# A dynamic convolution and a squared-ReLU feed-forward on one core: the order of the first loads, and block rows copied inside SBUF

## The chip, the cores and the metric

The kernel runs on one core of one Trainium2 chip. A core has five engines, each with its own queue of instructions that it works through in order: TensorE (PE) multiplies matrices, VectorE (DVE) and ScalarE (ACT) do elementwise work, GpSimd (POOL) does elementwise work and issues transfers, SyncE (SP) here issues transfers only. Transfers (DMAs) from SP go through one queue (q1 in the profile), those from POOL through another (q0); both are served by the same 16 DMA engines. SBUF is the on-chip memory with 128 partitions, PSUM is where PE writes, DRAM holds inputs and outputs. The metric is device time in microseconds (us) of one execution; lower is better.

## The reference

```python
# x: (8, 4096, 192), weight_gen: (8, 4096, 8 heads, 7 taps)
w = exp(weight_gen - max);  w = w / (sum(w) + 1e-9)        # softmax over the 7 taps
x_pad = 6 zero rows ahead of each sequence of x
out[b, s, h*24:(h+1)*24] = sum over k of w[b, s, h, k] * x_pad[b, s + k, h*24:(h+1)*24]
# then, on the 32768 rows of out, with w_in (192, 2048) and w_out (2048, 192):
h = maximum(out @ w_in, 0)
return (h * h) @ w_out
```

All inputs are 32-bit floats. The kernel computes in 16-bit floats with 32-bit sums.

## The kernel before

The 32768 rows are worked in 64 blocks of 512 rows (8 blocks to each of the 8 batches). A block goes through these steps:

- *Softmax.* `Softmax` (lines 138 to 210) handles a piece of one batch: `load` brings weight_gen to SBUF, `exp` (L172, ACT), `recip` (L180 and L185, DVE) and `scale` (L193, eight DVE instructions for a small piece) put the normalised taps into a tile `v`, `store` (L207, SP) writes the tile to a DRAM tensor `vd`. Batch 0 is split into three pieces, s0, s1 and s2, of 8, 8 and 16 rows on each of the 128 partitions: rows 0 to 1023, 1024 to 2047 and 2048 to 4095. Their tiles are `v_first[0]` to `v_first[2]`. Later batches are one piece (`v_big`), worked in slices during the blocks before.
- *Rows of taps.* A block's taps are needed in another layout, five tiles of 128 rows each (`wr`), whose tile i begins at row -24 + 104 i of the block. `wr_load` (L264) reads them from `vd` in DRAM; `wr_load_sbuf` (L269) copies them straight from an SBUF tile, one DMA for each of the five.
- *Bands.* `st_band` (L289, DVE) multiplies `wr` with a band mask into `bd`, the banded matrix of the convolution.
- *Convolution.* `st_conv` (L338, PE, 72 small matmuls of x by `bd`) writes `yp` in PSUM, `st_y_evac` (L351, ACT) copies it to SBUF as `y`.
- *Feed-forward.* For each of 8 groups fp: `st_mm1` (L363, 12 matmuls, PE), `st_relu` (L393, ACT), `st_sq` (L399, DVE); then `st_mm2` (L382, PE) with w_out, in two halves, G0 (fp 0 to 3) and G1 (fp 4 to 7). `o_copy` (L404) and `o_store` (L409) bring the result out.

PSUM: three buffers of two banks are shared in turn by the warm-up tile `wp`, `yp` and `h`, so a fourth group of mm1 waits until the first one's relu has read its buffer. `t` (relu's output) has five buffers.

The order of the work is written out by hand: each engine and each DMA queue takes its instructions in the order of the code. The head of the kernel, ahead of the loop over blocks (lines 452 to 495), is: 36 matmuls on zeros (`spin`, L441) while the first data arrive; loads on SP of s0's weights, of both halves of w_in (`load_w_in`, L114 and L115, in f32), of block 0's x (`x_load_f32`); softmax of s0; casts of w_in to f16 into `w_i` (L127: "straight" is slot 0 of the tile, the others are copies of 64 partitions to other slots and partitions) on ACT, POOL and DVE; rows of blocks 0 and 1 copied from s0's SBUF tile; loads of block 1's x and of w_out from POOL; bands and convolution of block 0, four more spins; s1's softmax; s1's store to DRAM; and the load of block 2's rows (`wr_load(2)`) from DRAM, which waits for that store. mm1 of groups 0 to 3 uses the first half of w_in, groups 4 to 7 the second.

In the loop, block 0 runs its groups 0 to 3, then block 1's convolution, block 2's bands, its groups 4 to 7, the first half of mm2, and part of s2's softmax. Block j's other half of mm2 stands in block j+1, behind block j+2's convolution.

Of the kernel before, what the change touches and what calls it, by code (L numbers as in the profile page):

```python
# [9 lines left out]
def kernel(  # L10
# [20 lines left out]
    nc = tc.nc  # L31
# [10 lines left out]
    P = 128  # L42
# [8 lines left out]
    HALO = KK - 1  # L51
# [5 lines left out]
    NT = 5  # L57
# [31 lines left out]
    v_first = [  # L89
        const.tile([P, r + 2 * HALO, HP, SL, 2], f16, name=f"v_first{i}")  # L90
        for i, r in enumerate(FIRST)
    ]
# [17 lines left out]
    def load_w_in(q):  # L110
        c = slice(q * NQ, (q + 1) * NQ)
        w_sa[q] = p_st.tile([P, NQ], f32, name="w_sa")
        w_sb[q] = p_st.tile([RT, NQ], f32, name="w_sb")
        nc.sync.dma_start(out=w_sa[q], in_=moe_w_in[0:P, c])  # L114
        nc.sync.dma_start(out=w_sb[q], in_=moe_w_in[P:D, c])  # L115

    def cast_w_in(q, op, copy):
        c = slice(q * NQ, (q + 1) * NQ)
        lower, upper = slice(0, RT), slice(RT, P)
        out_p, slot, src = {  # L120
            "straight": (slice(0, P), 0, w_sa[q]),
            "up": (upper, 1, w_sa[q][lower]),
            "down": (lower, 1, w_sa[q][upper]),
            "last": (lower, 2, w_sb[q]),
            "last up": (upper, 2, w_sb[q]),
        }[op]
        copy(out=w_i[out_p, slot, c], in_=src)  # L127
# [86 lines left out]
    def new_vd(b):  # L214
        vd_t[b] = p_dr.tile([S, H * SL], f16, name="vd")
        return vd_t[b]


    x_t, wr_t, bd_t, yp_t, y_t, g_t, h_t, t1_t, o_t, o_sb_t = ({} for _ in range(10))
# [32 lines left out]
    def x_load(j):  # L252
        x_t[j] = p_x.tile([P, NT, D], f16, name="xt")
        block_load(j, x_t[j], x[j // NBB], D, nc.gpsimd)
# [9 lines left out]
    def wr_load(j):  # L264
        wr_t[j] = p_wr.tile([P, NT, HP, SL * 2], f16, name="wr")
        wr = wr_t[j].rearrange("p t g c -> p t (g c)")
        block_load(j, wr, vd_t[j // NBB], H * SL, nc.sync)

    def wr_load_sbuf(j, s, order, engines):  # L269

        wr_t[j] = p_wr.tile([P, NT, HP, SL * 2], f16, name="wr")
        for n, i in enumerate(order):
            t0 = max(j * TB + tile_start(j, i), 0)
            engines[n % len(engines)].dma_start(  # L274
                out=wr_t[j][:, i].rearrange("p g c -> p (g c)"),
                in_=s.v[t0 // s.r : (t0 + P) // s.r, HALO : HALO + s.r].rearrange(
                    "p r g c e -> p r (g c e)"
                ),
            )

    def st_band(j, tiles):

# [65 lines left out]
    def st_y_evac(j):  # L348
        y = p_y.tile([P, NK, TH], f16, name="y")
        y_t[j] = y  # L350
        nc.scalar.copy(  # L351
            out=y, in_=yp_t[j][:, 0 : NK * TH].rearrange("p (k c) -> p k c", k=NK)
        )
# [41 lines left out]
    def st_sq(j, fp):  # L395
        g = p_g.tile([P, 2, 2, TH], f16, name="g")
        g_t[(j, fp)] = g
        t1 = t1_t[(j, fp)]
        nc.vector.tensor_tensor(out=g, in0=t1, in1=t1, op=AluOp.mult)  # L399
# [26 lines left out]
    with nc.allow_low_precision("fp16 matmul pipeline"), tc.manual_schedule():  # L426

        vd0 = new_vd(0)
        parts = [
            Softmax(0, P * sum(FIRST[:i]), r, v_first[i], vd0) for i, r in enumerate(FIRST)  # L430
        ]
        warm = const.tile([P, TB], f16, name="warm")
        nc.vector.memset(warm, 0.0)  # L433
        for i in (0, 1):
            nc.vector.memset(v_first[i], 0.0)

        wp = ps_h.tile([P, 2 * TB], f32, name="wp", tag="h")

        def spin(n):
            for i in range(n):  # L440
                nc.tensor.matmul(  # L441
                    out=wp[:, 0:TB], lhsT=warm[:, 0:P], rhs=warm, start=True, stop=True
                )

        def softmax(s, lo, hi):
            s.exp(lo, hi)
            s.recip(lo, hi)
            s.scale(lo, hi, nc.vector)

        vec, act, pool = nc.vector.tensor_copy, nc.scalar.copy, nc.gpsimd.tensor_copy  # L450
        s0, s1, s2 = parts
        spin(36)
        band_mask()
        s0.load(nc.sync)
        load_w_in(0)
        load_w_in(1)
        x_load_f32(0)
        s0.exp(0, s0.rh)
        s0.recip(0, s0.rh)
        s0.scale(0, s0.rh, nc.vector)  # L460
        cast_w_in(0, "straight", act)
        cast_w_in(0, "up", act)
        cast_w_in(0, "down", pool)
        cast_w_in(0, "last", act)
        cast_w_in(0, "last up", act)
        wr_load_sbuf(0, s0, (0, 1, 2, 4, 3), (nc.sync, nc.gpsimd))
        cast_w_in(1, "up", vec)
        cast_w_in(1, "down", vec)
        x_load(1)
        s1.load(nc.sync)  # L470
        for q in range(4):
            load_w_out(q, 4)
        nc.gpsimd.memset(v_first[2], 0.0)
        x_cast(0, act)
        wr_load_sbuf(1, s0, range(NT), (nc.sync,))
        s0.store(nc.sync)
        s2.load(nc.sync)
        cast_w_in(1, "straight", act)
        cast_w_in(1, "last", act)
        for i in (0, 2, 1, 3, 4):  # L480
            st_band(0, (i,))
        st_conv_alloc(0)
        st_conv(0)
        spin(4)
        s1.exp(0, s1.rh)
        st_y_evac(0)
        cast_w_in(1, "last up", act)
        x_load(2)
        nc.gpsimd.memset(v_big, 0.0)
        st_bands(1, 0)  # L490
        st_bands(1, 1)
        s1.recip(0, s1.rh)
        s1.scale(0, s1.rh, nc.vector)
        s1.store(nc.sync)
        wr_load(2)


        plan = {}

        def spread(b, rh, blocks):  # L500
            lo = 0
            for n, j in enumerate(blocks):
                left = len(blocks) - n
                hi = min(lo + -(-(rh - lo) // (UNIT * left)) * UNIT, rh)
                if lo < hi:
                    plan[j] = (b, lo, hi)
                lo = hi

        spread(0, s2.rh, (0, 1))
        for b in range(1, B):  # L510
            first = NBB * (b - 1)
            spread(b, R + HALO, range(first + (2 if b == 1 else -2), first + 5))
        rows_of = {0: s2}

        for j in range(NBLK):
            nb, lo, hi = plan.get(j, (None, 0, 0))
            after = plan.get(j + 1)
            if after and after[1] == 0:
                s = Softmax(after[0], 0, R, v_big, new_vd(after[0]))
                s.load(nc.sync)  # L520
                rows_of[after[0]] = s
            if j + 3 < NBLK:
                x_load(j + 3)

            late = j == 2
            if j:
                if j + 1 < NBLK:
                    st_conv_alloc(j + 1)
                    st_conv(j + 1)
                    st_y_evac(j + 1)  # L530
                if not late:
                    st_bands(j + 2, 0)
            for fp in G0:
                st_mm1(j, fp)
                st_relu(j, fp)
                st_sq(j, fp)
            if j:
                for half in (0, 1):
                    st_mm2(j - 1, G1, (half,))
                    o_copy(j - 1, half, nc.scalar.copy)  # L540
                o_store(j - 1, (0, 1), nc.sync)
            elif NBLK > 1:
                st_conv_alloc(1)
                st_conv(1)
                st_y_evac(1)
                st_bands(2, 0)
            if not late:
                st_bands(j + 2, 1)
            if hi and j:
                s = rows_of[nb]  # L550
                softmax(s, lo, hi)
                if hi == s.rh:
                    s.store(nc.sync)
            for fp in G1:
                st_mm1(j, fp)
                st_relu(j, fp)
                st_sq(j, fp)
            st_mm2(j, G0)
            if hi and not j:
                softmax(rows_of[nb], lo, hi)  # L560
            if late:
                st_bands(j + 2, 0)
                st_bands(j + 2, 1)
            if j + 3 < NBLK:
                wr_load(j + 3)
        st_mm2(NBLK - 1, G1, (0,))
        o_copy(NBLK - 1, 0, nc.scalar.copy)
        st_mm2(NBLK - 1, G1, (1,))
        o_store(NBLK - 1, (0,), nc.sync)
        o_copy(NBLK - 1, 1, nc.vector.tensor_copy)  # L570
        o_store(NBLK - 1, (1,), nc.scalar)
# [30 lines left out]
```

## Time and profile before

| | us |
|---|---|
| median of 4 runs | 794.53 |
| lowest, highest | 792.83, 795.98 |
| the profiled execution | 793.45 |
| its span, first to last instruction | 791.7 |
| PE busy in the span | 772.7 (98%) |
| ACT, DVE, POOL busy | 610.4, 584.5, 73.5 |

A line of a timeline gives the start and the duration in us, the engine, the line of the kernel, the operation, the tile written and the tile read, and how many instructions are merged; the bracket at its end says how long the engine had been idle and what ended that. DMA landings, where a text gives them, are the times at which the DMA's semaphore got its increments from the 16 engines, in the same trace; the last of the 16 counts.

### The profile page before, as it was taken

Reading aid. Unit: us, or ns where it says so; the run is one execution under the profiler, and the core shown is the slowest. Engines: PE = TensorE matmul, PEld = TensorE weight load, DVE = VectorE, ACT = ScalarE, POOL = GpSimd, SP = SyncE. Lnnn points to the kernel's source line nnn. Section 1 sums busy time; section 2 is a strip of 40 time slices with the busy share of each in tenths; the row PEclk is TensorE's granted clock in tenths of the full one; section 3 lists DMA queues with packets and bytes.
Section 4 is the critical chain, followed back from the end, with each engine's and each line's share of the span. In section 5 each row is a group of like instructions: output and inputs, shape, how many; then the busy total and the mean of one; then the engine's idle time right before and its main releaser. Section 6 shows DMA issues by size and latency. Waiting matters only on the chain.

```text
span 791.7 us, 32661 instructions
## 1 busy us (share of the span) xinstructions
PE 772.7 (98%) x14888; PEld 679.3 (86%) x14888; DVE 584.5 (74%) x1042; ACT 610.4 (77%) x761; POOL 73.5 (9%) x96
## 2 busy tenths in 40 slices
PE   7698999999999999999999999999999999999998
PEld 3587888888888888888888988888888888889887
DVE  5688778776887768777778777877778777667653
ACT  6586877877877877877877877877787787787785
POOL 7201000010001000010001000011000010000000
PEclk9899999999999999999999999999999999999999
DMA  9932633435433453435433453333533333342111
GB/s 200 177 78 39 154 55 64 75 51 146 76 52 65 97 110 64 75 52 145 76 51 66 72 133 68 71 54 68 149 61 65 65 64 83 70 70 45 50 42 41
DMA packets 123929, 64.09 MB, mean 81 GB/s; under 512 B 87281, under 2 KB 121104, under 8 KB 123024
## 3 DMA queue, kind: packets, MB, share of 16 engines
q1 hardware_dynamic: 79744, 45.51, 20.8%
q0 software_dynamic: 43776, 16.31, 19.4%
q8 instruction: 116, 1.90, 1.0%
q10 hardware_dynamic: 272, 0.20, 0.1%
q14 instruction: 21, 0.17, 0.1%
HBM read 48.74 MB, written 29.36 MB: 99 GB/s over the span
## 4 chain that ended last, share of the span: by engine, by line
PE 94%; DVE 2%; DMA 2%; SPq 1%; ACT 0%; issue 0%; DVEq 0%
PE o L382 44%; PE h L363 43%; PE yp L338 7%; DMA wr<-v_first 1%; DVE bd L289 1%; SPq L274 1%; DMA vd<-v_first 1%; DVE v_first L193 0%; DMA wg<-in_weight_gen_dram 0%; DVE ssum L180 0%; DVE rcp L185 0%; DVE g L399 0%; ACT ex L172 0%; DMA wr<-vd 0%; DVE v_big L193 0%
## 5 line engine op out<-in xcount | busy, mean ns | idle before, releaser
L393 ACT ACTIVATE t<-h 128x1024 f16<-128x1024 f32 x512 | 482.7, 1030 | 10.4 <-PE h L363 8.3
L399 DVE TENSOR_TENSOR g<-t 128x1024 f16<-128x1024 f16 x512 | 345.1, 690 | 143.8 <-ACT t L393 143.6
L363 PE MATMUL h<-y,w_i 64*128 64x256 f16 x6144 | 361.7, 270 | 0.6 <-ACT t L393 0.3
L382 PE MATMUL o<-w_o,g 128*128 128x192 f16 x4096 | 360.0, 246 | 0.7 <-DVE g L399 0.7
L382 PEld LDWEIGHTS <-g 128*128 128x128 f16 x4096 | 331.5, 98 | 27.6 <-DVE g L399 17.9
L363 PEld LDWEIGHTS <-w_i 64*128 64x128 f16 x6144 | 292.0, 94 | 49.4 <-issue 12.3
L289 DVE TENSOR_TENSOR bd<-wr,mask 128x1664 f16<-128x1664 f16 (+2 forms) x201 | 160.8, 831 | 18.5 <-DMA wr<-vd 12.3
L351 ACT CAST y<-yp 128x768 f16<-128x768 f32 x64 | 51.0, 798 | 121.3 <-PE yp L338 121.3
L250 POOL DMA_DIRECT2D xt<-in_x_dram x63 | 52.1, 828 | 472.9 <-PE yp L338 447.2
L404 ACT COPY o_sb<-o 128x384 f32<-128x384 f32 x127 | 62.9, 495 | 38.2 <-PE o L382 38.0
L338 PE MATMUL yp<-bd,xt 128*32 128x104 f16 (+12 forms) x4608 | 60.6, 203 | 12.6 <-DVE bd L289 9.2
L338 PEld LDWEIGHTS <-xt 128*32 128x32 f16 (+3 forms) x4608 | 51.5, 91 | 23.9 <-issue 20.2
L180 DVE TENSOR_REDUCE ssum<-ex 128x64 f32<-128x448 f32 (+6 forms) x49 | 25.9, 529 | 32.7 <-ACT ex L172 32.7
L193 DVE TENSOR_TENSOR v_big<-ex,rcp 128x112 f16<-128x112 f32 (+3 forms) x192 | 32.8, 235 | 1.6
L172 ACT ACTIVATE ex<-wg 128x448 f32<-128x448 f32 (+6 forms) x49 | 26.5, 541 | 1.9 <-DMA wg<-in_weight_gen_dram 1.9
L185 DVE RECIPROCAL rcp<-ssum 128x64 f32<-128x64 f32 (+6 forms) x49 | 23.3, 476 | 1.7
L244 POOL DMA_DIRECT2D xt<-in_x_dram x10 | 5.7, 575 | 88.4 <-PE yp L338 88.4
L441 PE MATMUL wp<-warm 128*128 128x512 f16 x40 | 11.7, 460 | 1.3 <-DVE warm L433 1.3
L240 POOL DMA_DIRECT2D xt<-in_x_dram x7 | 3.8, 541 | 77.4 <-PE yp L338 77.4
L441 PEld LDWEIGHTS <-warm 128*128 128x128 f16 x40 | 4.3, 112 | 7.4 <-issue 3.2
L193 DVE TENSOR_TENSOR v_first<-ex,rcp 128x112 f16<-128x112 f32 (+2 forms) x32 | 6.3, 270 | 0.2
L127 ACT CAST w_i<-w_sa 128x1024 f16<-128x1024 f32 (+1 forms) x3 | 3.1, 1043 | 1.9 <-DMA w_sa<-in_moe_w_in_dram 1.9
(19 smaller groups left out, 22.9 us busy)
## 6 DMA issues: line engine op xcount, KB each, us to landing
out_dram<-o_sb SPq DMA_DIRECT2D x63, 384.0 KB, 2.8
xt<-in_x_dram POOLq DMA_DIRECT2D x46, 240.0 KB, 4.2
wg<-in_weight_gen_dram SPq DMA_DIRECT2D x6, 1064.0 KB, 5.7
wr<-vd SPq DMA_DIRECT2D x46, 80.0 KB, 3.0
vd<-v_big SPq DMA_DIRECT2D x7, 512.0 KB, 3.3
xt<-in_x_dram POOLq DMA_DIRECT2D x17, 192.0 KB, 3.9
w_sa<-in_moe_w_in_dram SPq DMA_DIRECT2D x2, 512.0 KB, 6.8
wr<-vd SPq DMA_DIRECT2D x16, 64.0 KB, 3.0
```

What stands on the lines that cost most here:

```text
L172: nc.scalar.activation(out=self.ex[:, lo:hi].rearrange("p r g k e -> p (r g) k e"), in_=self.wg[:, lo:hi].rearrange("p r (g e) k -> p (r g ...
L180: nc.vector.tensor_reduce(out=ssum.rearrange("p r g e -> p (r g) e"), in_=self.ex[:, lo:hi].rearrange("p r g k e -> p (r g) e k"), axis=Ax ...
L193: eng.tensor_tensor(out=bass.AP(tensor=v.tensor, offset=v.offset + lo * H * SL + lo % SL * 2 + g * SL * 2, ap=[list(v.ap[0]), [H * SL + 2, ...
L250: eng.dma_start(out=dst[:, first:last], in_=ap)
L289: nc.vector.tensor_tensor(out=bd_t[j][:, H * lo : H * hi].rearrange("p (g m c) -> p g m c", g=shape[1], c=2 * SL), in0=wr_t[j][:, i : tile ...
L338: nc.tensor.matmul(out=yp_t[j][p0 : p0 + m, col + a : col + b], lhsT=x_t[j][:, i, 32 * q : 32 * q + m], rhs=bd[:, h // 2, h % 2, a - lo : ...
L351: nc.scalar.copy(out=y, in_=yp_t[j][:, 0 : NK * TH].rearrange("p (k c) -> p k c", k=NK))
L363: nc.tensor.matmul(out=h[:, half, jj, :], lhsT=w_i[r0 : r0 + RT, slot, fc * P : (fc + 1) * P], rhs=y_t[j][r0 : r0 + RT, k, :], start=(jj = ...
L382: nc.tensor.matmul(out=o[half][:, cc * Dm : (cc + 1) * Dm], lhsT=g_t[(j, fp)][:, half, jj, cc * P : (cc + 1) * P], rhs=w_o[:, fc, :], star ...
L393: nc.scalar.activation(out=t1, in_=h_t[(j, fp)], func=ActF.Relu)
L399: nc.vector.tensor_tensor(out=g, in0=t1, in1=t1, op=AluOp.mult)
L404: copy(out=o_sb_t[j][:, half], in_=o_t[j][half][:, 0 : 2 * Dm])
```

## The change

The first load of x moves ahead of the second half of w_in, and that half's load moves behind the copies of block 0's rows on SP's queue. The copies of block 1's rows move ahead of s1's load. The casts of w_in's second half move behind block 0's evacuation, "straight" on ACT and the four others on POOL. `spin` has 42 matmuls. `wr_load_sbuf` takes several pieces and copies a tile from each piece that it overlaps; block 2's rows are copied with it from s0's and s1's tiles (tile 0 from both, so six DMAs), in place of the load from DRAM. s1's reduce and reciprocal stay in the head; its scale, these copies and its store follow the second square of block 0.

```diff
-    def wr_load_sbuf(j, s, order, engines):
+    def wr_load_sbuf(j, parts, order, engines):
 
         wr_t[j] = p_wr.tile([P, NT, HP, SL * 2], f16, name="wr")
-        for n, i in enumerate(order):
+        n = 0
+        for i in order:
             t0 = max(j * TB + tile_start(j, i), 0)
-            engines[n % len(engines)].dma_start(
-                out=wr_t[j][:, i].rearrange("p g c -> p (g c)"),
-                in_=s.v[t0 // s.r : (t0 + P) // s.r, HALO : HALO + s.r].rearrange(
-                    "p r g c e -> p r (g c e)"
-                ),
-            )
+            for s in parts:
+                a, b = max(t0, s.t0), min(t0 + P, s.t0 + P * s.r)
+                if a < b:
+                    engines[n % len(engines)].dma_start(
+                        out=wr_t[j][a - t0 : b - t0, i].rearrange("p g c -> p (g c)"),
+                        in_=s.v[
+                            (a - s.t0) // s.r : (b - s.t0) // s.r, HALO : HALO + s.r
+                        ].rearrange("p r g c e -> p r (g c e)"),
+                    )
+                    n += 1
...
-        spin(36)
+        spin(42)
         band_mask()
         s0.load(nc.sync)
         load_w_in(0)
-        load_w_in(1)
         x_load_f32(0)
...
         cast_w_in(0, "last", act)
-        cast_w_in(0, "last up", act)
-        wr_load_sbuf(0, s0, (0, 1, 2, 4, 3), (nc.sync, nc.gpsimd))
-        cast_w_in(1, "up", vec)
-        cast_w_in(1, "down", vec)
+        wr_load_sbuf(0, [s0], (0, 1, 2, 4, 3), (nc.sync, nc.gpsimd))
+        load_w_in(1)
         x_load(1)
+        wr_load_sbuf(1, [s0], range(NT), (nc.sync,))
         s1.load(nc.sync)
         for q in range(4):
             load_w_out(q, 4)
-        nc.gpsimd.memset(v_first[2], 0.0)
         x_cast(0, act)
-        wr_load_sbuf(1, s0, range(NT), (nc.sync,))
+        cast_w_in(0, "last up", act)
         s0.store(nc.sync)
         s2.load(nc.sync)
-        cast_w_in(1, "straight", act)
-        cast_w_in(1, "last", act)
         for i in (0, 2, 1, 3, 4):
             st_band(0, (i,))
         st_conv_alloc(0)
         st_conv(0)
         spin(4)
+        st_y_evac(0)
+        cast_w_in(1, "straight", act)
+        cast_w_in(1, "up", pool)
+        cast_w_in(1, "down", pool)
+        cast_w_in(1, "last", pool)
+        cast_w_in(1, "last up", pool)
         s1.exp(0, s1.rh)
-        st_y_evac(0)
-        cast_w_in(1, "last up", act)
+        nc.gpsimd.memset(v_first[2], 0.0)
         x_load(2)
         nc.gpsimd.memset(v_big, 0.0)
         st_bands(1, 0)
         st_bands(1, 1)
         s1.recip(0, s1.rh)
-        s1.scale(0, s1.rh, nc.vector)
-        s1.store(nc.sync)
-        wr_load(2)
+
+        def rest_of_s1():
+            s1.scale(0, s1.rh, nc.vector)
+            wr_load_sbuf(2, [s0, s1], range(NT), (nc.sync,))
+            s1.store(nc.sync)
...
                 st_sq(j, fp)
+                if (j, fp) == (0, 1):
+                    rest_of_s1()
```

## The prediction

> **What bounds the kernel now.** I read the page first: share of busy time, then the chain that ended last.
>
> ```profile
> PE 772.7 (98%) x14888; PEld 679.3 (86%) x14888; DVE 584.5 (74%) x1042; ACT 610.4 (77%) x761; POOL 73.5 (9%) x96
> ...
> PE 94%; DVE 2%; DMA 2%; SPq 1%; ACT 0%; issue 0%; DVEq 0%
> ```
>
> TensorE (PE) is the bound: 94% of the chain is matmuls, and nothing the change touches makes them fewer. What is left for it is the head, where the chain runs over other engines. So next the timeline of the first 40 us (start, duration, instruction, idle before it and who ended that), which shows where PE stands still:
>
> ```profile
> 14.16 1.03 PE L338 MATMUL yp<-bd,xt 128*32 128x104 f16 x26 [3.10 <-ACT xt L262]
> ...
> 22.62 0.56 DVE L289 TENSOR_TENSOR bd<-wr,mask 128x768 f16<-128x768 f16 x1 [2.11 <-DMA wr<-v_first]
> ...
> 23.23 0.44 PE L338 MATMUL yp<-bd,xt 128*32 128x96 f16 x22 [1.06 <-DVE bd L289]
> ...
> 24.98 1.46 DVE L193 TENSOR_TENSOR v_first<-ex,rcp 128x112 f16<-128x112 f32 x8
> ...
> 27.09 2.81 PE L382 MATMUL o<-w_o,g 128*128 128x192 f16 x32 [0.69 <-DVE g L399]
> ...
> 32.70 2.43 DVE L289 TENSOR_TENSOR bd<-wr,mask 128x1664 f16<-128x1664 f16 x3 [3.85 <-DMA wr<-vd]
> ...
> 33.87 0.27 PE L338 MATMUL yp<-bd,xt 128*32 128x104 f16 x2 [3.96 <-DVE bd L289]
> 34.71 1.46 PE L338 MATMUL yp<-bd,xt 128*32 128x56 f16 x70 [0.57 <-DVE bd L289]
> ```
>
> Two holes matter: 3.10 us before block 0's convolution, and 3.96 + 0.57 us before block 2's. The second follows from one path: s1's scale ends at 26.44, its store lands in DRAM at 30.55 (15 of 16 engines at 28.82), the load of block 2's rows is issued at 30.61 and lands at 32.67, then bands. The chain in order of time says the same:
>
> ```profile
> 24.98 1.47 DVE v_first L193 x8
> 26.46 4.09 DMA vd<-v_first
> 30.58 0.03 issue
> 30.61 2.07 DMA wr<-vd
> 32.70 1.97 DVE bd L289 x2
> ```
>
> The stages of this stretch (window: us, PE busy, PEld, DVE, ACT, POOL, granted PE clock, DMA share, GB/s) show a second price of the hole, the clock:
>
> ```profile
> 30.00:32.00 2.00, 0.00 (x0) 0.00 (x0) 0.00 (x0) 0.70 (x1) 0.00 (x0) 1.00 0.17 28
> 32.00:34.00 2.00, 0.13 (x2) 0.14 (x3) 1.30 (x2) 0.00 (x0) 0.00 (x0) 0.59 0.88 120
> 34.00:36.00 2.00, 1.43 (x72) 1.23 (x69) 2.00 (x4) 0.00 (x0) 0.00 (x0) 0.50 0.84 328
> 36.00:38.00 2.00, 2.00 (x29) 1.36 (x20) 2.00 (x4) 1.19 (x2) 0.84 (x1) 0.50 0.40 161
> ```
>
> Block 1's first 48 matmuls of L363 take 4.28 us from 36.11 at half clock; the same 48 take 2.79 at 23.61. From 40.32 on (the product with w_out of block 0's second half) PE has no hole until 63.87, and that one is set by work that starts after an output copy of PE's own. So a shift of 40.32 goes to the end whole, and **the forecast is that shift**.
>
> **The change, part by part.** *x_st before w_in(1).* x_st landed at 13.04, after w_in's second half (11.59); between 8.23 and 11.59 the queue moved that half, 3.4 us. Moved ahead, x_st lands near 9.7 (8.23 + its own 1.45). Block 0's five row copies, issued from 9.20 on, landed 13.22 to 13.94, right behind x_st; with an empty queue they land 2.0 us after issue (as the 2.07 of wr<-vd), at 11.2 to 12.5. Bands (five, 2.57 busy) end near 14.1 instead of 15.89, block 0's convolution ends near 14.5 to 15 instead of 16.66. Gain 1.6 us there, if what follows keeps it.
>
> *spin(42).* Six more matmuls of 0.213 are 1.3 us, from 11.06 to 12.35, inside the hole that remains. Cost nothing; if the bands came before 12.3, at most 1.3.
>
> *w_in(1) now stands on SP's queue behind block 0's copies*, and s1.load, which was issued at 11.18 and landed at 14.70, stands behind w_in(1) and block 1's five copies. This is the term that decides. On ScalarE (ACT), in order, s1.exp stands ahead of block 0's first relu; so that relu waits for s1.load, and behind it the other relus and block 1's evacuation (PE waits for both, for PSUM buffers), and on DVE s1's reduce with the squares behind it. Call the landing L.
> w_in(1) is issued at 11.18, moves from about 12.3 (first load: issued 0.80, moving at 1.9). Alone, 768 KB took 3.4 us; beside POOL's queue (20 to 24 us) SP's queue moved 0.76 MB in 4.0 us. 1.6 us of the one and 2.1 of the other: landed at 16.0. Block 1's five copies took from 14.70 to 20.80 beside w_out and x: 6.1 us. POOL has the same loads to make here (x_load(1) and w_out, 2688 packets; about 630 of them by 16.0, the rest at the 407 per us that it made from 14 to 20), so it runs dry around 21, and I put 5.5 to 6.1: 21.5 to 22.1. s1.load itself: 392 KB, 1.3 us as before or 2.1 at the crowded rate. L = 22.8 to 24.2; I take **23.5**. Ends: copies uncrowded, 0.18 us apart as block 0's were, give 16.0 + 0.9 + 1.3 = 18.2; the slowest engine's lag (1.8 us on the last copy, 20.80 to 22.60, 3.4 on the last w_out piece, 21.58 to 25.02) gives 24.2 + 3.4 = 27.6. I stand by the middle because it is the same five copies against the same queue.
> The Trainium skill, "DMA: Bandwidth & Descriptors", section on queues, rings and completion order, says that each engine takes turns between the queues with work, a packet at a time. The row above it: from 14 to 20 us SP's queue moved 702 packets and POOL's 2440, no equal turns. With equal turns the copies' 640 packets would take some 2.4 us and L would be an estimated 19.8; I keep the row.
>
> *From L on* (durations from the rows): exp 0.93, reduce 0.96, reciprocal 0.85: L + 2.8. Two squares, which the change puts here, 2 x 0.62: L + 4.1 (their relus end by L + 2.9). Scale 1.46: L + 5.6. Six copies for block 2 on SP, 0.64 each (L274 took 0.60 and a gap of 0.04): tile 1, the third, leaves at L + 6.9, lands 2.07 later, L + 9.0; tile 3 at L + 10.3. Bands: 1.0 each, the second ends at L + 11.3, the last at L + 11.9. Convolution of block 2, 0.92 at full clock, ends about L + 12.4; 48 matmuls of L363, 2.79: L + 15.2. POOL's x_load(5), which was done by 28, now falls beside the copies: 0 to 1 us, taken 0.5, since DMA there is otherwise idle. Total L + 15.7 = 39.2, against 40.32: **1.1 us gained**. From scale to convolution's end the new way costs 6.8 instead of 9.7 (36.17 - 26.44); what it gains, s1's late arrival eats: before, the scale ended at 26.44, now at L + 5.6 = 29.1.
> Lag of the last engine on L is likely in part; half its smaller size, 0.9, once in two: 0.4. Net **0.7 us gained**.
>
> *PE beside this.* It stops after three of four mm1 groups of block 0 (three PSUM buffers), near 17.5 to 18, until the relu at L + 1.96: a hole of 7.5 us in place of those above, and the clock falls. In this trace PE restarts at 14.16 and 33.87 got full clock 4.6 and 5.3 us later; so here at L + 7. Rest of mm1 (1.4 cold), convolution of block 1 (1.7 cold), four mm1 groups (one cold, three warm, 3.5), mm2 (2.81): L + 1.96 + 9.4 = L + 11.4, just under the bands' L + 11.9. If the clock came two us later, up to 1.3 us more.
>
> *Casts of w_in(1).* DVE loses two (1.47 us, from idle time), ACT keeps one, POOL gets four, 1.12 each as its one now: from 15 to about 20.5; used at L + 5. Behind them on POOL: v_first memset, x_load(2) (16.69, now about 22.5), v_big memset, x_load(3) (19.91, now about 26); x is needed at 34 and 48; landing takes 3.8. Covered by over 7 us. A POOL cast beside DVE's scale made it 2.30 instead of 1.46; here bands of block 1 run beside, which wait for copies and then for s1 anyway: 0, at worst 0.8.
>
> *SP's tail.* s0.store and s2.load move behind s1.load; s2.exp, at 29.86 before, now comes after L + 10, and 616 KB land by L + 5. s1.store is issued behind the six copies, near L + 9.5; block 3's rows land some 5 us later, bands for it at about 41; batch 1's weights (issued at 32.07, 5.4 to land) leave near 36 and are used at 55.5. All covered by 2 us or more.
>
> **The sum.** The profiled run took 793.45 us (span 791.7 and 1.75 around it): 793.45 - 0.7 = 792.75. The median of four runs is 1.08 higher, so 793.8. A measurement of this kernel tells from no change about 0.3%, 2.4 us.
>
> **Rivals.** *A, faster:* s1.load is not last, because the copies are less crowded (w_out's 1.5 MB is held up by w_in(1), x_load(2) not yet issued). For: POOL's queue runs dry near 21. Against: 6.1 us for the same copies now. With L at 21.0: 21.0 + 15.2 to 15.7 = 36.2 to 36.7, 3.6 to 4.1 us faster, 790.4 to 790.9. It passes 2.4 us at L below 22.2.
> *B, slower:* one DMA engine lags, and s1.load, at the end of the row, waits for it, with relu, squares and block 2 behind it. For: 22.60 against 20.80, 25.02 against 21.58, 30.55 against 28.82. Against: 14.70 and 19.39 landed with their fellows, and the POOL queue drains earlier here. L = 27.5 gives 43.2, 2.9 us slower: 797.4. It decides above L = 27.0.
> *C, nothing of it is seen:* block 2's rows come earlier, but PE's own cold work is the bound: with the clock two us later its mm2 ends at L + 12.7 and the convolution at L + 13.6 instead of 12.4, which makes 0.7 faster into 0.5 slower, inside no change.
>
> **How the numbers follow.** Forecast with C (L 22.2 to 27): 0.52, of its own 792.1 to 796.5. A 0.25, B 0.23. The range runs to the rivals' values, 790.4 to 797.5. Same comes from the forecast, faster from A, slower from B.
>
> **What would show it.** Right: s1.exp released by its DMA near 23.5, relu of block 0 after it; PE idle 7 us before 26; the bands of block 2 released by wr<-v_first at L + 9; full clock at block 1's mm1, 48 in about 2.8. Wrong: s1.exp before 21, or PE waiting for something other than the relu there; copies for block 2 landing later than 4 us after issue; a POOL cast that mm1 waits for.

## The result and the profile after

The changed kernel takes 794.86 us (median of 53 runs) against 793.61 before (79 runs): ratio 1.0018, 95% interval 1.0010 to 1.0026, so slower by some 1.4 us. The forecast was 0.7 us faster and called it no change that can be told; the size is inside that, the sign is not. The 2.4 us that the prediction took for the smallest difference a measurement can tell was too much: with these numbers of runs the interval is 0.6 us to either side.

The page of the kernel after, share of busy time and the chain that ended last:

```profile
PE 772.3 (98%) x14894; PEld 679.1 (86%) x14894; DVE 582.8 (74%) x1040; ACT 608.2 (77%) x759; POOL 77.5 (10%) x100
...
PE 93%; DVE 3%; DMA 2%; issue 1%; SPq 0%; ACT 0%; DVEq 0%
```

PE does the same work. Its chain lost one per cent to DVE and to issue time, all of it in the head. The timeline of the first 45 us, with the lines that answer to those shown of before:

```profile
14.23 0.91 PE L343 MATMUL yp<-bd,xt 128*32 128x104 f16 x46 [0.71 <-DVE bd L294]
...
23.43 0.94 ACT L172 ACTIVATE ex<-wg 128x784 f32<-128x784 f32 x1 [5.49 <-DMA wg<-in_weight_gen_dram]
...
25.33 1.47 PE L368 MATMUL h<-y,w_i 64*128 64x256 f16 x12 [7.15 <-ACT t L398]
...
27.32 1.45 DVE L193 TENSOR_TENSOR v_first<-ex,rcp 128x112 f16<-128x112 f32 x8
...
35.47 2.43 DVE L294 TENSOR_TENSOR bd<-wr,mask 128x1664 f16<-128x1664 f16 x3 [5.50 <-DMA wr<-v_first]
...
36.64 0.23 PE L343 MATMUL yp<-bd,xt 128*32 128x104 f16 x2 [2.37 <-DVE bd L294]
...
37.48 0.91 PE L343 MATMUL yp<-bd,xt 128*32 128x56 f16 x70 [0.61 <-DVE bd L294]
...
38.32 2.79 PE L368 MATMUL h<-y,w_i 64*128 64x256 f16 x48
```

The 3.10 us hole before block 0's convolution is gone, and block 0's convolution ends 1.5 us earlier (15.14 against 16.66). Then ACT waits 5.49 us for s1's weights, PE 7.15 us behind it, and block 2's bands, the aim of the copies, start at 35.47, not earlier than before (32.70) but 2.8 us later. The chain says where that comes from:

```profile
27.40 1.37 DVE v_first L193 x8
28.77 0.61 DVE g L404
29.38 0.31 SPq L278
29.69 0.05 issue
29.74 5.60 DMA wr<-v_first
```

Tile 1's copy, 16 KB inside SBUF, leaves at 29.74 and lands at 35.34. What was 4.09 (store) + 2.07 (load) over DRAM is now 5.60 in one step, and the scale ahead of it ends at 28.77 instead of 26.44. The clock gives part of it back: the stages, in the same columns as before, show full clock where before had 0.50 to 0.59, and PE idle for most of 34 to 38.

```profile
32.00:34.00 2.00, 2.00 (x27) 2.00 (x25) 0.00 (x0) 2.00 (x3) 0.00 (x0) 1.00 1.54 192
34.00:36.00 2.00, 0.26 (x4) 0.03 (x1) 0.54 (x1) 0.08 (x1) 0.00 (x0) 1.00 0.20 52
36.00:38.00 2.00, 0.75 (x51) 0.65 (x55) 2.00 (x4) 0.00 (x0) 0.00 (x0) 1.00 0.23 37
```

So block 2's convolution ends 2.2 us later (38.39 against 36.17) than before, block 1's first 48 matmuls take 2.79 instead of 4.28, and the second half of block 0's mm2 starts at 41.05 against 40.32. That 0.7 us then stays: the last block's convolution comes 0.76 later in this profile. The profiled executions differ by 0.4 us (793.82 and 793.45), the medians by 1.25; profiles are single executions. The one of the change had a granted clock of 0.995, more than most of its runs (median 0.991); what runs differ by is told below.

### The profile page after: what moved, and what is told of

The parts are those of the page before. It is cut to its first block, busy times and chain, and to the rows that moved or that the text cites. A ratio compares the mean times of both kernels' runs of the same rounds, so it can differ in the third digit from the quotient of the medians.

```text
span 792.1 us, 32681 instructions
## 1 busy us (share of the span) xinstructions
PE 772.3 (98%) x14894; PEld 679.1 (86%) x14894; DVE 582.8 (74%) x1040; ACT 608.2 (77%) x759; POOL 77.5 (10%) x100
## 4 chain that ended last, share of the span: by engine, by line
PE 93%; DVE 3%; DMA 2%; issue 1%; SPq 0%; ACT 0%; DVEq 0%
PE o L387 44%; PE h L368 43%; PE yp L343 7%; DMA wr<-v_first 2%; DVE bd L294 1%; DVE g L404 1%; DVE v_first L193 0%; DMA wg<-in_weight_gen_dram 0%; DVE ssum L180 0%; SPq L278 0%; DVE rcp L185 0%; ACT ex L172 0%; DVE v_big L193 0%; ACT t L398 0%; SPq L114 0%
## 5 line engine op out<-in xcount | busy, mean ns | idle before, releaser
L368 PE MATMUL h<-y,w_i 64*128 64x256 f16 x6144 | 361.5, 270 | 7.7 <-ACT t L398 7.5
L368 PEld LDWEIGHTS <-w_i 64*128 64x128 f16 x6144 | 291.8, 94 | 55.8 <-issue 19.1
L294 DVE TENSOR_TENSOR bd<-wr,mask 128x1664 f16<-128x1664 f16 (+2 forms) x201 | 161.3, 834 | 23.5 <-DMA wr<-v_first 14.7
L446 PE MATMUL wp<-warm 128*128 128x512 f16 x46 | 12.4, 433 | 1.3 <-DVE warm L438 1.3
```

The costliest lines, as they stand in the source:

```text
L294: nc.vector.tensor_tensor(out=bd_t[j][:, H * lo : H * hi].rearrange("p (g m c) -> p g m c", g=shape[1], c=2 * SL), in0=wr_t[j][:, i : tile ...
L368: nc.tensor.matmul(out=h[:, half, jj, :], lhsT=w_i[r0 : r0 + RT, slot, fc * P : (fc + 1) * P], rhs=y_t[j][r0 : r0 + RT, k, :], start=(jj = ...
```

## The experiments

The theory after reading: *late copies*. Block 2's copies are late because x_load(3), (4) and (5), issued from POOL between 26.98 and 30.0, are moved at the same time, and they stand there because POOL first casts w_in's second half, for which it waits. Rivals: *late s1* (s1.load decides all that follows), *clock* (the long PE hole costs half-clock time in the typical run, more than in the profiled one), *copies in SBUF are slow in themselves*, and *the slowest engine's instruction fetch* instead of the loads. Times are ratios to the kernel before, run on the same chip; the change's own ratio, 1.0018, is the one above, and a difference to the change is the difference of the two ratios.

**s1's load first.**

```diff
+        s1.load(nc.sync)
         load_w_in(1)
         x_load(1)
         wr_load_sbuf(1, [s0], range(NT), (nc.sync,))
-        s1.load(nc.sync)
```

> Only s1.load's place on SP's queue changes (ahead of w_in's second half and block 1's copies). Late-copies theory (the loss is in block 2's copies, which crowd with POOL's late x loads; block 1's rows are as late as s1): s1.exp at about 19 instead of 23.43, the PE hole of 7.15 us before 25.33 shrinks to some 4 us, but bands of block 1 still end near 24.5 to 25.5, scale near 28.5 to 29.5 and block 2's bands start within 1 us of 35.47; time within 1 us of the changed kernel. Late-s1 theory (L decides all): scale 3 to 4 us earlier, block 2's bands at about 32, time 3 us lower. Clock theory (the long PE hole decides how many half-clock windows a run has): granted clock higher than the 0.991 of the typical run, median 1 to 2 us lower even with the bands no earlier.

Measured: 1.0052 (1.0034 to 1.0070), that is some 2.7 us slower than the change. s1's exp runs at 19.96 instead of 23.43, and PE's hole shrinks from 7.15 to 3.83. But block 1's bands and the scale move back by 1 us, and block 2's bands by more:

```profile
28.35 1.45 DVE L193 TENSOR_TENSOR v_first<-ex,rcp 128x112 f16<-128x112 f32 x8
...
36.85 1.03 DVE L294 TENSOR_TENSOR bd<-wr,mask 128x1664 f16<-128x1664 f16 x1 [5.85 <-DMA wr<-v_first]
38.23 1.50 DVE L294 TENSOR_TENSOR bd<-wr,mask 128x1664 f16<-128x1664 f16 x2 [0.36 <-DMA wr<-v_first]
```

Late s1 falls: the load came, and the scale did not. In the changed kernel the bands of block 1 end at 24.45 and s1's exp at 24.37, two limits at one time. My expectation of no change within 1 us missed too: w_in's second half now landed at 18.98 and 21.31 (16.88 and 19.98 in the change), so POOL's casts ended at 24.17 (22.17), x_load(3) left at 28.99 (26.98), and the copies took 5.6 us from issue to landing (median; 4.7 in the change).

**The copies alone.** The kernel before, with `wr_load_sbuf` for several pieces and

```diff
-        s1.scale(0, s1.rh, nc.vector)
-        s1.store(nc.sync)
-        wr_load(2)
+        def rest_of_s1():
+            s1.scale(0, s1.rh, nc.vector)
+            wr_load_sbuf(2, [s0, s1], range(NT), (nc.sync,))
+            s1.store(nc.sync)
...
+                if (j, fp) == (0, 1):
+                    rest_of_s1()
```

> The kernel before with one part of the change: block 2's rows copied in SBUF, and s1's scale behind the second square; head, loads and casts as before, so POOL's x loads land by 29. Late-copies theory: scale ends at 27.7 (26.44 + 1.24), the copies land 2 to 2.5 us after issue, bands of block 2 start at about 31 instead of 32.70 and end at 34, PE reaches block 1's mm1 at about 34.7 instead of 36.11; 1 to 2.5 us faster than before. Theory that copies inside SBUF are slow in themselves: bands no earlier than 33.5, time same or slower than before.

Measured: 0.9958 (0.9937 to 0.9979), 3.3 us faster. Timeline, DVE and PE:

```profile
23.08 1.45 DVE L193 TENSOR_TENSOR v_first<-ex,rcp 128x112 f16<-128x112 f32 x8
...
28.53 2.43 DVE L294 TENSOR_TENSOR bd<-wr,mask 128x1664 f16<-128x1664 f16 x3 [2.80 <-DMA wr<-v_first]
```

Scale's end to bands: 4.0 us, against 6.3 before and 6.7 in the change. The four whole copies landed 1.9 to 2.9 us after issue. So copies inside SBUF are not slow in themselves. More was gained in this profile than expected (block 1's mm1 at 31.95, 4.2 us earlier than before) because block 1's last copy landed at 19.58 here and at 22.60 in the profile of before, where one engine lagged; the head varies by that much between runs.

**Fewer x loads beside the copies.**

```diff
-    p_x = ctx.enter_context(tc.tile_pool(name="p_x", bufs=4))
+    p_x = ctx.enter_context(tc.tile_pool(name="p_x", bufs=2))
```

> The changed kernel with two buffers for x instead of four: x_load(3) waits for block 1's convolution, and x_load(4) and x_load(5) for later ones, so one load (640 packets) instead of three stands beside block 2's copies. Late-copies theory: bands of block 2 start at 32.5 to 34 instead of 35.47, PE's hole of 2.37 + 0.61 us before block 2's convolution all but closes, time 1.5 to 3 us below the changed kernel. Clock theory: less cold work only by the smaller second hole, at most 1 us. Theory that the slow engine's instruction fetch, not the loads, made the copies late: bands at 35 to 35.5, no change.

Measured: 0.9979 (0.9967 to 0.9991), 3 us below the change. **Casts off POOL:**

```diff
-        cast_w_in(1, "up", pool)
-        cast_w_in(1, "down", pool)
-        cast_w_in(1, "last", pool)
-        cast_w_in(1, "last up", pool)
+        cast_w_in(1, "up", act)
+        cast_w_in(1, "down", act)
+        cast_w_in(1, "last", act)
+        cast_w_in(1, "last up", act)
```

> The changed kernel with the four casts of w_in's second half on ACT instead of POOL, in the time in which ACT waits for s1 (17.9 to 23.4), so that POOL issues x_load(2) at about 17 and x_load(3), (4) at about 20 to 21 instead of 23.8 to 29. If POOL's casts are what brings the x loads beside the copies: copies land 1.5 to 3 us earlier (bands of block 2 at 32.5 to 34), time 1 to 3 us below the changed kernel. If the loads only queue longer behind w_out and land no earlier: bands within 0.7 us of 35.47, no change. If the earlier x loads hold up s1.load instead: s1.exp after 24.5, and the gain is lost.

Measured: 0.9991 (0.9977 to 1.0006), some 2 us below the change. Both do the same thing to the DMA queues while the copies run. First the change (DMA view of 29 to 34 us: packets and MB of each queue, q0 is POOL's and q1 SP's; then KB and median us to landing):

```profile
q0 software_dynamic: 1819, 0.68, 121.8%
q1 hardware_dynamic: 659, 0.12, 15.3%
...
wr<-v_first SPq DMA_DIRECT2D x4, 16.0 KB, 4.7
```

The same view with two x buffers:

```profile
q0 software_dynamic: 672, 0.25, 48.1%
q1 hardware_dynamic: 837, 0.21, 20.5%
...
wr<-v_first SPq DMA_DIRECT2D x4, 16.0 KB, 2.5
```

and with the casts on ACT:

```profile
q0 software_dynamic: 774, 0.29, 53.1%
q1 hardware_dynamic: 837, 0.21, 18.4%
...
wr<-v_first SPq DMA_DIRECT2D x4, 16.0 KB, 2.5
```

With 1819 packets of POOL's in the window the copies take 4.7 us, with 672 or 774 they take 2.5, by whichever way the packets went. These medians leave out tile 1, whose landing is what the bands wait for: it took 5.60 us in the change and 3.34 in each of the other two. The number of packets in a window is not by itself the measure, though. In the kernel with the copies alone POOL's queue moved 1506 packets from 24 to 29 us, and the copies were quick:

```profile
q0 software_dynamic: 1506, 0.56, 95.6%
...
wr<-v_first SPq DMA_DIRECT2D x4, 16.0 KB, 1.9
```

What goes with the landing is the time at which POOL's queue runs dry. With the copies alone its packets fell from 414 between 26 and 27 us to 98 in the next microsecond, and tile 1 landed at 28.41. With two x buffers and with the casts on ACT they fell to 13 and 6 in the microsecond after 32 (tile 1 at 32.65 and 32.88), in the change to 30 in the one after 34 (35.34, 15 of 16 engines at 33.93).

With two x buffers and with the casts on ACT, block 2's bands start at 32.77 and 33.00 (35.47 in the change), with the scale's end within 0.5 us of the change's in both, and block 1's mm1 starts at 35.63 and 35.87 (38.32). The instruction fetch (one DMA of 16 KB, 1.1 to 1.4 us on one engine near 28) is there with two x buffers too, at 27.9, and the last engine lands within 0.14 us of the others; in the change it was 1.4 us behind on tile 1 (33.93 and 35.34). So the lag alone is not the cause, though about 1.4 of the 2.9 us that tile 1 was late against the forecast is the last engine, behind a queue that was full. In this profile, ACT took four casts at no cost: it waited 0.77 us for s1 instead of 5.49.

**Block 2 over DRAM again, in the new head.**

```diff
-            wr_load_sbuf(2, [s0, s1], range(NT), (nc.sync,))
             s1.store(nc.sync)
+            wr_load(2)
```

> The changed kernel with block 2's rows loaded from DRAM again, behind s1's store. Late-copies theory (the head's new order is what costs, the copies themselves gain even when crowded): scale ends at 28.8 as there, the store lands at 34 to 36 beside POOL's x loads, block 2's load 2 us later, bands at 36.5 to 38, time 1 to 2.5 us above the changed kernel. Rival (copies inside SBUF are worse than the way over DRAM): bands at 35 or earlier, time at or below the changed kernel.

Measured: 1.0067 (1.0044 to 1.0089). Bands at 36.18, after scale's end at 28.33. So the change is two opposite parts, with the scale's later place in both: the head's new order costs 5.3 us, the copies alone gain 3.3, and both together cost 1.4 (the parts add up to 2.0, which the intervals allow). The copies gain in either head.

**The clock.** 31 matmuls on zeros into a free bank, while PE waits for s1:

```diff
                 st_mm1(j, fp)
+                if (j, fp) == (0, 2):
+                    spin(31, wq)
```

> The changed kernel with 31 matmuls on zeros (0.216 us each, 6.7 us) between mm1 groups 2 and 3 of block 0, into a bank that is free then, so that PE is not idle for 7.15 us. Clock theory: no half-clock windows after 16 us, granted clock near 0.997 in most runs, median 1 to 2.5 us lower and the spread of the runs (791.8 to 799.2) half as wide. Late-copies theory alone: mm1, convolution of block 1 and mm2 end 2 us earlier, but block 2's bands are still at 35.5, so a profile like the one of the change (two cold windows) gets no faster, within 0.5 us.

Measured: 1.0023 (1.0005 to 1.0041), as the change. The profile has full clock to 65 us, and the spins fill the hole:

```profile
17.77 6.86 PE L448 MATMUL o<-warm 128*128 128x512 f16 x31
24.98 0.83 PE L368 MATMUL h<-y,w_i 64*128 64x256 f16 x12 [0.34 <-ACT t L398]
```

Block 2's bands still come at 34.31, PE waits 2.56 us for them, and nothing is won in time. The runs' granted clock rose (median 0.9955 against 0.991), as the clock theory expected, but their time did not fall, and they lie between 791.97 and 798.68, not half as wide as before the spins (791.8 to 799.2). So filling that hole does not bring the loss back. It does not clear the clock as a whole: in this profile block 1's mm1 starts at 37.17 instead of 38.32, and half clock then comes behind a later hole instead, near 65 us, where 48 matmuls took 4.46 us instead of 2.79.

The clocks on record with the runs settle a part of the rest. At equal granted clock the median of the change lies above that of the kernel before by 1.6 us at 0.989 (10 runs of the change, 12 of before), by nothing at 0.991 (21 and 6), by 1.4 at 0.993 (11 and 16) and by 0.6 at 0.995 (6 and 8). So in three of the four groups a loss is there at the same clock too. The change's runs also have a somewhat lower clock (median 0.991 against 0.993), and how much of the 1.4 us comes from that is not shown.

**Better versions.** The copies alone, with POOL's and SP's queue taking turns at the six copies (x_load(4) and (5) then stand behind them on POOL), and the same with two x buffers:

```diff
-            wr_load_sbuf(2, [s0, s1], range(NT), (nc.sync,))
+            wr_load_sbuf(2, [s0, s1], range(NT), (nc.gpsimd, nc.sync))
```

> The kernel before with the copies alone (the second run here), the six copies now shared by POOL's and SP's queue; x_load(4) and x_load(5) come behind them on POOL. If issue time and crowding are what is left between scale and bands: bands of block 2 start at 27 to 27.7 instead of 28.53, last copy lands 1 us earlier, time 0.5 to 2 us below that run's 789.6. If POOL's own way to issue is slower: bands at 28.5 or later, no change.

> The same with two buffers for x instead of four. x_load(4) and (5) already stand behind the copies on POOL, so crowding theory expects no more than 0.5 us of difference to the run with four buffers; if fewer buffers cost something later in the blocks, block to block times (11.78 and 11.89 us) grow and it is slower by more than 2 us.

Measured: 0.9946 (0.9926 to 0.9967) and 0.9950 (0.9930 to 0.9969), medians 788.86 and 789.20. Both beat both kernels. Against the copies on SP alone (0.9958) the intervals overlap, so the second queue's gain is not shown in time. The bands, expected at 27 to 27.7, started at 28.53, which was the sign of the theory that POOL's way to issue is slower, so that theory stays open. In the profile bands start 2.4 us after the scale's end instead of 4.0, at the same 28.53, because the scale came later in that run (it ended at 26.16 instead of 24.53); and the last copy, expected 1 us earlier than the 29.78 with SP alone, on SP behind five others, landed at 31.34. Two x buffers change nothing more, as expected.

## Why the prediction was wrong

- *The head's own steps came out as forecast.* x_st at 9.7: 9.91. Block 0's convolution done at 14.5 to 15: 15.14. Block 1's copies at 21.5 to 22.1: 21.90. The deciding term L, s1's landing, 23.5: 23.41. PE's hole of 7.5: 7.15. Scale's end, L + 5.6 = 29.0: 28.77. The clock back near L + 7 = 30.4: 29.39. That L came out right is in part luck: w_in's second half landed at 19.98 instead of 16.0, and block 1's copies were all in 1.9 us after it, at 21.90, instead of the 5.5 to 6.1 of the sum, so two misses of some 4 us cancelled.
- *The term that failed* is the one called "POOL's x_load(5), ... 0 to 1 us, taken 0.5, since DMA there is otherwise idle". It was not one load but three, and tile 1's copy took 5.60 us from issue to landing where the sum has 2.07. With the measured L it was forecast to land at L + 9.0 = 32.4 and landed at 35.34, although it left 0.6 us earlier than forecast. Block 2's convolution, forecast at L + 12.4 = 35.8, ended at 38.4. That is 2.6 us, 2.1 more than the 0.5 in the sum. Taking the crowd away brought 2 to 3 us in two ways. That 2.1 us is also what lies between the forecast (0.7 faster) and the measurement (1.4 slower) is partly chance: in the profiles the start at 40.32 was forecast to come 1.1 us earlier and came 0.7 later, 1.8 us off, and the medians hold what the granted clock does to the runs as well.
- *Why it failed.* The paragraph on casts priced POOL's late x loads against the blocks that need the data ("covered by over 7 us") and stopped there. It had their issue times nearly right (22.5 and 26, measured 23.76 and 26.98), and the copies' times right (issued from 29), and did not lay the two beside each other. x_load(4) was not named at all. The reading behind the 0.5 was off as well: in the trace of before x_load(5) was not done by 28, it landed at 30.16 (15 of 16 engines at 28.47).
- *A smaller miss ahead of it:* w_in's second half was put at 16.0 and landed at 16.88 and 19.98. From 16 to 20 us SP's queue moved 0.31 MB beside x_load(1) and w_out, where the crowded rate in the sum was 0.76 MB in 4.0 us. That made POOL's casts end at 22.17 instead of 20.5 and the x loads 1 us later still.
- *Missed in the other direction:* the first of the six copies, tile 0's part from s0, does not need s1's scale; it left at 20.38, so five issues were left behind the scale instead of six.
- *From scale to convolution's end, "6.8 instead of 9.7"* was right for the mechanism and holds where nothing crowds it: 7.5 in the kernel with the copies alone, against 9.6 in the change.
- *Of the rivals,* A needed block 1's copies to come earlier than 21.9, and they did not; with s1 first the time rose. B had the right direction and the wrong transfer: the lag came on block 2's copies, not on s1.load. C's bound did not bind: PE ended mm2 at 34.3 and waited for bands.
- *The rule of equal turns* (the Trainium skill, "DMA: Bandwidth & Descriptors", the section on queues, rings and completion order), which the prediction set aside for its row, is neither shown nor refuted by these counts. Over the whole stretch from 29 to 34 us POOL's queue moved 1819 packets and SP's 659, but the share moved: 480 to 18 from 31 to 32 us, 393 to 200 in the next microsecond and 337 to 441 from 33 to 34. When SP's queue had work waiting on every engine, the trace does not say. The same holds for the prediction's 702 and 2440.

## What to carry to other kernels

When a change moves transfers later, price them twice: against whoever needs their data, and against every short transfer that will now be in the queues at the same time. Here a 16 KB copy took 1.9 to 2.9 us while POOL's queue was running dry, and 4.2 to 5.6 beside a stream of casting loads, and these small copies on the critical chain were what cost time, not the large loads. Waits on an engine that also issues DMAs (here casts on POOL) move all the DMAs behind them; with the casts on ACT, which issues none here and waited anyway, the time fell by some 2 us. And try the parts of a combined change one at a time, since here one part alone is worth 3.3 us and the other costs 5.3.

## What the runs showed of the hardware

Runs of one kernel differ along with the granted clock. Of the changed kernel's runs, the six at 0.995 have a median of 792.45 us, the ten at 0.989 one of 797.11. In the clock records of these traces half-clock time comes in stretches of 3.41, 6.83 or 10.24 us (but for the one that each trace ends in), and the traces show one place for it that no kernel here touched: PE waits 2.73 + 0.62 us for block 4's bands, near 60 us, and after that hole block 3's 48 matmuls of L368 took 2.79 us in the change and in the kernel before, but 3.47 to 4.88 in the eight other kernels:

```profile
64.59 0.23 PE L343 MATMUL yp<-bd,xt 128*32 128x104 f16 x2 [2.73 <-DVE bd L294]
...
66.27 2.79 PE L368 MATMUL h<-y,w_i 64*128 64x256 f16 x48
```

Those are the change; the next are the change with two x buffers:

```profile
61.89 0.27 PE L343 MATMUL yp<-bd,xt 128*32 128x104 f16 x2 [2.74 <-DVE bd L294]
...
64.13 4.88 PE L368 MATMUL h<-y,w_i 64*128 64x256 f16 x48
```

The same wait cost nothing in one execution and more than 2 us in another. This is more than the effect that was forecast, so one profile of each kernel can show the reverse of what the medians do; whether a head that ends at another time makes the loss likelier was not tried. Behind that place all kernels run alike: from block 6's convolution to block 63's the traces differ by at most 0.4 us.

A second source of scatter is the head itself: with the same code ahead of it, block 1's last copy landed at 22.60 in the profile of before and between 19.58 and 20.71 in the kernels that share its head up to there, with one engine 1.8 us behind the others in the first and 0.15 in the earliest.
